# Walking the inner dimension of a fused attention and gated-MLP kernel in pairs of tiles

## The chip, the cores and the metric

One core of one Trainium2 chip runs the whole kernel in one launch. The metric is the device time in microseconds. A profile of one further execution gives the busy times, waits and transfers. Five engines run side by side: TensorE (PE, with its weight loads shown as PEld), VectorE (DVE), ScalarE (ACT), GpSimd (POOL) and SyncE (SP, which here only issues transfers).

## What is computed

Inputs are q, k and v for 8 batches, 8 heads, 576 positions and 64 features per head, and three weight matrices. Cut to what matters:

```python
# attention: a coarse part on means over 4 positions, and a local band of 7 positions
q_d, k_d, v_d = means of q, k, v over 4 neighbouring positions       # 144 positions
out_up    = repeat(softmax(q_d k_d^T / 8) v_d, 4)
out_local = softmax(mask(q k^T / 8, |i - j| < 4)) v
x = (out_up + out_local) as 4608 tokens of 512 features
# gated MLP
xn  = x / sqrt(mean(x^2) + 1e-6) * rms_g
g   = xn @ w_gate            # 512 x 1536
val = xn @ w_val             # 512 x 1536
out = (g * sigmoid(g) * val) @ w_out      # 1536 x 512
```

The weights arrive as 64-bit floats, which the kernel decodes on the chip.

## The kernel before

**Tokens.** The 4608 tokens are worked on in 18 chunks of 256 (C). For each chunk the class `Attention` computes the local band, adds the coarse result, normalises, and transposes the chunk on TensorE (`turn`, L907) into two tiles, `xh` (L911, ACT) and `xl` (L915, DVE): a rounded part and the remainder. Both come from the pool `xp`, with 2 buffers of each name. The class `Coarse` computes the coarse attention for two heads of one batch at a time; there are 32 such steps.

**The MLP.** The class `Forward` walks the inner dimension of 1536 in 12 tiles f of 128 (NF). For each f and each chunk:

- `first(f, 0)` and `first(f, 1)` (L976): 12 products of 128x256 each, which give gate and value in the two halves of one PSUM tile `ps_h` of 128x512 (3 buffers, one bank each);
- `tanh` (L983, ACT), `gate` (L986, DVE), `product` (L991, DVE), each on 128x256;
- `high` (L997, ACT) writes a rounded copy into the tile `hs`, `low` (L1000, DVE or POOL) the remainder;
- `second` (L1011): 6 products of 128x512 into two accumulators `ps_o`. It runs LAG = 2 tiles behind.

After f = 11 the two accumulators are copied (L1018) and stored (L1021). The buffers are `sil` 3 and `hs` LAG + 1 = 3.

**The weights.** Each of 36 pieces (512 KB of raw 64-bit numbers) goes through `fetch` (SP, L250), `scale` (ACT, L254, takes one of 4 `o_sb` buffers), `last_bits` (POOL, L264), `join` (DVE, L271), `high` (ACT, L281 or L283) and `split` (DVE, L293 or L295, or POOL, L291), which frees the `o_sb` buffer. A piece is of no use before all of these. 32 pieces are fetched into memory that later holds other weights; the pieces 28, 31, 34 and 35 are fetched into one extra tile `raw` of the pool `stage`, which holds one piece at a time. A staging place is free again after `join`. Pieces 24 to 31 hold the gate and value weights of the last four tiles f.

**What sets the order.** The opening is ordered by a planner written into the kernel (class `Plan`). Every step is a task with an engine, a cost, a due time and the buffers that it takes (`allocs`) or uses. At each turn the planner takes the task that can start earliest on its engine, and among those within 0.15 of it the one with the earliest due time. A task that takes a buffer can be picked only when all users of the buffer's earlier holder are planned (`room`). The instructions of each engine then stand in the planned order, in-order on the chip. The planner orders the opening attention, the weight pieces, and the chunks 0 to 2; from chunk 3 on a loop writes out one f after the other, with the steps of the next chunk's `Attention` and of `Coarse` placed between them at fixed fractions.

Three more places matter for what follows:

- `OpeningSums` adds up the sums for the coarse attention of the first two batches. For batch 1 it takes its results' places from the pools of the main loop: `xh` and `xl` for q and k (`load_qk`, `copy`, L420), two `hs` buffers for v (`add_v`, L429). The raw v lies where gate weights will be written, so the `high` step of gate and value pieces waits for the last `add_v`.
- `warm_up` (L1102) fills an `hs` buffer, on which 30 products without use (`idle_product`, L1105) keep TensorE busy. They are planned with the latest due times of all, so they run when TensorE has nothing else.
- `Attention.plan`: `turn(0)` takes `xh` and `xl`; the sums that chunk 1 makes on TensorE (`value_sum`, L827) wait for chunk 0's `turn`.

Of the kernel before, what the change touches and what calls it, by code (L numbers as in the profile page):

```python
# [8 lines left out]
FP32 = mybir.dt.float32  # L9
# [10 lines left out]
P = 128  # L20
# [13 lines left out]
US = 4  # L34
# [4 lines left out]
WPC = 512  # L39
LAG = 2  # L40
W_BUFS = 4
# [30 lines left out]
class Plan:  # L72
# [6 lines left out]
    def buf(self, res):  # L79
        return Buf(res)  # L80
# [90 lines left out]
def attn_moe_kernel(  # L171
# [73 lines left out]
    def load_weight(src, hi_lo, f, n, gain, k):  # L245
        st = {}

        def fetch(place):
            raw = st["raw"] = place if place is not None else stage.tile([P, WPC, 2], U32, name="raw")
            return nc.sync.dma_start(out=raw, in_=src.bitcast(U32).rearrange("p (n t) -> p n t", t=2)).ins  # L250
# [56 lines left out]
    def load_second(f):  # L307
# [56 lines left out]
    class OpeningSums:  # L364
# [57 lines left out]
        def add_v(self, j, engine):  # L422
            if j == 1:
                if self.b:
                    self.vs = ffn.tile([HALF, 4, 2, D], FP32, name="hs", bufs=LAG + 1)
# [3 lines left out]
            (nc.gpsimd if engine == "POOL" else nc.vector).tensor_tensor(  # L429
                out=vs, in0=self.raw_v[:, 0] if j == 1 else vs, in1=self.raw_v[:, j], op=ALU.add,  # L430
            )
# [153 lines left out]
    class Attention:  # L585
# [55 lines left out]
        def plan(self, newton="POOL", before=()):  # L641
# [98 lines left out]
        def load_score(self, j, par):  # L740
            k = load_kv(k_pad, 2 * self.c + j, par)
            if self.c == 0 and j == 1:
                q = ffn.tile([P, US, D], FP32, name="sil", bufs=3)
            else:
                q = loads.tile([P, US, D], FP32, name="q_t", bufs=2)
# [172 lines left out]
    class Forward:  # L918


        def __init__(self, att):
            self.att, self.c = att, att.c
            self.p, self.sil, self.hs, self.o_sb = {}, {}, {}, {}

        def emit(self, f):
            self.first(f, 0)
            self.first(f, 1)
            self.tanh(f)
            self.gate(f)
            self.product(f)  # L930
            self.high(f)
            self.low(f, "DVE")

        def emit_second(self, f):
            self.second(f)
            if f == NF - 1:
                for j in range(2):
                    self.copy(j)
                    self.store(j)

        def plan(self, weights, second_weights):
            att, c, T = self.att, self.c, due[self.c]
            o_bufs = [buf("ps_o") for _ in range(2)]
            last = None
            for f in range(NF):
                at = T + 4.2 * f
# [3 lines left out]
                first = task(  # L950
                    "PE", 1.375, lambda f=f: self.first(f, 0), at, [*att.turned, *weights(f)], allocs=[hp], uses=x,
                )
                tanh = task("ACT", 0.38, lambda f=f: self.tanh(f), soon, [first], allocs=[sil], uses=[hp])
                val = task("PE", 1.375, lambda f=f: self.first(f, 1), at, [first], uses=[hp, *x])
                gate = task("DVE", 0.415, lambda f=f: self.gate(f), soon, [tanh], uses=[hp, sil])
                prod = task("DVE", 0.415, lambda f=f: self.product(f), soon, [gate, val], uses=[hp, sil])
                high = task("ACT", 0.415, lambda f=f: self.high(f), soon, [prod], allocs=[hs], uses=[sil])
                low = task(
                    (("DVE", 0.42, soon), ("POOL", 0.95, soon)), 0, lambda e, f=f: self.low(f, e), soon, [high], uses=[sil, hs],
                )  # L960
                last = task(
                    "PE", 1.375, lambda f=f: self.second(f), at + 4.2 * LAG, [low, last, *second_weights(f)],
                    allocs=o_bufs if f == 0 else [], uses=[hs, *o_bufs],
                )
            for j in range(2):
# [3 lines left out]

        def first(self, f, t):  # L970
            if t == 0:
                self.p[f] = ps_h.tile([P, 2, C], FP32, name="ps_h")
            n, w = 0, (wg, wv)[t]
            for k in range(KT):
                for wi, xi in ((w[0], self.att.xh), (w[0], self.att.xl), (w[1], self.att.xh)):
                    nc.tensor.matmul(  # L976
                        out=self.p[f][:, t], lhsT=wi(f)[:, 0, k], rhs=xi[:, k], start=(n == 0), stop=(n == 3 * KT - 1),
                    )
                    n += 1

        def tanh(self, f):
            self.sil[f] = ffn.tile([P, C], FP32, name="sil", bufs=3)
            nc.scalar.activation(out=self.sil[f], in_=self.p[f][:, 0], func=AF.Tanh, scale=0.5)  # L983

        def gate(self, f):
            nc.vector.scalar_tensor_tensor(  # L986
                out=self.sil[f], in0=self.sil[f], scalar=1.0, in1=self.p[f][:, 0], op0=ALU.add, op1=ALU.mult,
            )

        def product(self, f):  # L990
            nc.vector.scalar_tensor_tensor(  # L991
                out=self.sil[f], in0=self.sil[f], scalar=0.5, in1=self.p[f][:, 1], op0=ALU.mult, op1=ALU.mult,
            )

        def high(self, f):
            self.hs[f] = ffn.tile([P, 2, C], FP32R, name="hs", bufs=LAG + 1)
            nc.scalar.activation(out=self.hs[f][:, 0], in_=self.sil[f], func=AF.Copy)  # L997

        def low(self, f, engine):
            (nc.gpsimd if engine == "POOL" else nc.vector).tensor_tensor(  # L1000
                out=self.hs[f][:, 1], in0=self.sil[f], in1=self.hs[f][:, 0], op=ALU.subtract,
            )

        def second(self, f):
            if f == 0:
                self.o = [ps_o.tile([P, DM], FP32, name="ps_o") for _ in range(2)]
            hh, hl = self.hs[f][:, 0], self.hs[f][:, 1]
            for j in range(2):
                cols = slice(j * P, (j + 1) * P)
                for i, (lhs, rhs) in enumerate(((hh, wo[0]), (hh, wo[1]), (hl, wo[0]))):  # L1010
                    nc.tensor.matmul(  # L1011
                        out=self.o[j], lhsT=lhs[:, cols], rhs=rhs(f)[:, 0],
                        start=(f == 0 and i == 0), stop=(f == NF - 1 and i == 2),
                    )
# [26 lines left out]
    spots = [f"first{n % 8}" for n in range(24)]  # L1041
    spots += ["second0", "second1", "second2", "second3", "stage", "second0", "second1", "stage"]
    spots += ["second2", "second3", "stage", "stage"]
    joined, whole = [], {}

    def decode(n):
# [4 lines left out]
        got = task(  # L1051
            "SP", 0.1, lambda: fetch(spot and spot[0].raw_place(*spot[1:])), at - 15, allocs=[raw],
            dma=0.524 * MB,
# [71 lines left out]
    for c in range(FIRST, NCH):  # L1125
# [10 lines left out]
        fwd = Forward(att)  # L1136
        for f in range(NF):
# [66 lines left out]
```

## Time and profile before

| What | Value |
|---|---|
| Time, median of 3 runs | 1144.62 us (1144.13 to 1148.87) |
| Span of the profiled execution | 1142.6 us |
| What lies around the span, against the median | 2.0 us |
| TensorE busy | 1080.1 us (95%) |
| VectorE busy | 963.1 us (84%) |
| ScalarE busy | 625.7 us (55%) |
| GpSimd busy | 173.0 us (15%) |
| First product of the MLP | at 107.84 us |
| Last copy out of the accumulators | at 1138.6 us |

No own time is listed for the profiled execution beside its span, so the median less the span stands for what lies around it.

How to read it: "L976" is line 976 of the kernel. A row of a group of instructions gives the line, the engine, the operation, output and inputs with their shapes, the count, then busy time and mean duration of one, then the engine's idle time before them and what ended it. A row of waits gives who waited for whom, the total, the number of times and the longest. A row of the timeline gives start and duration. A row of the table by stretches gives the length, then for each engine busy time and number of instructions, then the TensorE clock that was granted (1.00 is full), the share of the transfer engines and GB/s.

### The profile page before, as it was taken

The numbers are of one execution on the slowest core, as the hardware profiler recorded it, in microseconds if no ns is written. First come the engines' busy times: TensorE is split into PE (matmuls) and PEld (weight loads), VectorE is DVE, ScalarE is ACT, GpSimd is POOL, SyncE is SP. The second block draws the span as 40 slices with busy tenths as digits, with TensorE's granted clock in tenths as the row PEclk, the third lists the DMA queues.
The fourth block names the chain that finished last, engine by engine and source line by source line (L and its number), as shares of the span: only waits on it lengthen the run. The fifth ranks groups of instructions, "written<-read, shape, count | busy, mean of one in ns | idle before, by whom it ended". The sixth has DMA issues, their size and how long they took to land.

```text
span 1142.6 us, 21949 instructions
## 1 busy us (share of the span) xinstructions
PE 1080.1 (95%) x8002; PEld 987.1 (86%) x8002; DVE 963.1 (84%) x1869; ACT 625.7 (55%) x2284; POOL 173.0 (15%) x205
## 2 busy tenths in 40 slices
PE   6883799999999999999999999999999999999998
PEld 4772688878898899999999999998999999999997
DVE  6786998788999989797989797979898989997432
ACT  1564663847383847474747474747465573838221
POOL 1654662334200010101010101000000000000000
PEclk8875999999999899999999999999999999999999
DMA  9986482446544443535253535222231313220000
GB/s 267 300 274 173 107 222 84 96 95 148 124 100 105 110 104 88 115 88 115 83 120 88 114 88 114 78 63 76 65 89 54 99 52 99 67 60 20 1 19 20
DMA packets 76813, 119.57 MB, mean 105 GB/s; under 512 B 26784, under 2 KB 36256, under 8 KB 76704
## 3 DMA queue, kind: packets, MB, share of 16 engines
q1 hardware_dynamic: 47520, 97.34, 28.8%
q0 software_dynamic: 8640, 15.93, 9.1%
q10 hardware_dynamic: 20544, 4.89, 2.0%
q8 instruction: 63, 1.03, 0.4%
q14 instruction: 46, 0.38, 0.1%
HBM read 106.33 MB, written 11.80 MB: 103 GB/s over the span
## 4 chain that ended last, share of the span: by engine, by line
PE 78%; DVE 8%; DMA 7%; ACT 2%; issue 2%; POOL 1%; SPq 0%; ACTq 0%; DVEq 0%; POOLq 0%
PE ps_h L976 48%; PE ps_o L1011 24%; PE ps_a L541 2%; PE ps_a L499 2%; DMA wg<-in_v_sum_dram 1%; DMA wg<-in_w_gate_dram 1%; DVE o_sb L271 1%; PE ps_a L907 1%; DMA qk<-in_qk_sum_dram 1%; DMA kv<-in_k_pad_dram 1%; DVE prod L812 1%; PE ps_a L527 1%; DVE prod L758 1%; ACT up_t L856 1%; ACT prod L805 1%
## 5 line engine op out<-in xcount | busy, mean ns | idle before, releaser
L1011 PE MATMUL ps_o<-wo,hs 128*128 128x512 f32 x1296 | 355.7, 399 | 5.4 <-POOL hs L1000 5.3
L976 PE MATMUL ps_h<-xh,wg 128*128 128x256 f32 x1728 | 349.1, 282 | 4.0 <-DVE wg L295 1.7
L976 PE MATMUL ps_h<-xh,wv 128*128 128x256 f32 x1728 | 341.8, 280 | 5.0 <-DVE sil L986 4.9
L976 PEld LDWEIGHTS ps_h<-xh,wg 128*128 128x128 f32 x1728 | 284.0, 190 | 13.0 <-ACT xh L911 2.2
L976 PEld LDWEIGHTS ps_h<-xh,wv 128*128 128x128 f32 x1728 | 280.5, 188 | 11.0 <-DVE sil L986 6.9
L805 ACT ACTIVATE prod<-kv,sc 128x64 f32<-128x64 f32 x1072 | 279.2, 405 | 18.1 <-DVE x_t L831 9.8
L1011 PEld LDWEIGHTS ps_o<-wo,hs 128*128 128x128 f32 x1296 | 221.2, 188 | 43.1 <-POOL hs L1000 8.4
L976 PE MATMUL ps_h<-xl,wg 128*128 128x256 f32 x864 | 243.5, 282 | 0.1
L976 PE MATMUL ps_h<-xl,wv 128*128 128x256 f32 x864 | 241.8, 280 | 0.0
L983 ACT ACTIVATE sil<-ps_h 128x256 f32<-128x256 f32 x216 | 82.4, 382 | 227.8 <-PE ps_h L976 216.0
L986 DVE SCALAR_TENSOR_TENSOR sil<-sil,ps_h 128x256 f32<-128x256 f32 x216 | 91.1, 422 | 94.9 <-ACT sil L983 83.5
L976 PEld LDWEIGHTS ps_h<-xl,wg 128*128 128x128 f32 x864 | 164.0, 190 | 6.9 <-DVE sil L986 1.3
L976 PEld LDWEIGHTS ps_h<-xl,wv 128*128 128x128 f32 x864 | 163.0, 189 | 1.6
L997 ACT ACTIVATE hs<-sil 128x256 fp32r<-128x256 f32 x216 | 89.3, 415 | 133.9 <-DVE sil L991 112.3
L758 DVE TENSOR_TENSOR prod<-q_t,kv 128x896 f32<-128x896 f32 x140 | 153.1, 1094 | 5.7 <-DMA q_t<-in_q_band_dram 5.4
L762 DVE TENSOR_REDUCE sc<-prod 128x14 f32<-128x896 f32 x144 | 155.3, 1085 | 0.4
L831 DVE TENSOR_REDUCE x_t<-prod 128x128 f32<-128x896 f32 x128 | 135.7, 1080 | 11.5 <-PE ps_a L907 4.5
L812 DVE TENSOR_TENSOR prod<-sc,kv 128x384 f32<-128x384 f32 (+2 forms) x144 | 119.6, 868 | 0.2
L1000 DVE TENSOR_TENSOR hs<-sil,hs 128x256 fp32r<-128x256 f32 x196 | 87.3, 447 | 23.3 <-ACT hs L997 23.2
L991 DVE SCALAR_TENSOR_TENSOR sil<-sil,ps_h 128x256 f32<-128x256 f32 x216 | 91.2, 422 | 6.4 <-PE ps_h L976 4.8
L362 POOL DMA_DIRECT2D qk<-in_qk_sum_dram x36 | 32.2, 894 | 319.6 <-DMA qk<-in_qk_sum_dram 275.1
L856 ACT ACTIVATE up_t<-x_t 128x128 f32<-128x128 f32 x144 | 44.2, 307 | 21.3 <-DVE x_t L846 12.7
(118 smaller groups left out, 974.7 us busy)
## 6 DMA issues: line engine op xcount, KB each, us to landing
kv<-in_k_pad_dram SPq DMA_DIRECT2D x72, 320.0 KB
kv<-in_v_pad_dram SPq DMA_DIRECT2D x72, 320.0 KB
qk<-in_qk_sum_dram POOLq DMA_DIRECT2D x36, 288.0 KB, 5.0
out_dram<-o_sb SPq DMA_DIRECT2D x36, 256.0 KB
q_t<-in_q_band_dram SPq DMA_DIRECT2D x70, 128.0 KB
vs<-in_v_sum_dram POOLq DMA_DIRECT2D x36, 144.0 KB, 3.6
qk<-in_qk_sum_dram SPq DMA_DIRECT2D x12, 288.0 KB
wo<-in_qk_sum_dram SPq DMA_DIRECT2D x2, 1152.0 KB
```

Source lines behind the costliest of these rows:

```text
L758: nc.vector.tensor_tensor(out=pr, in0=bcast(q[:, s0:s0 + 2], 2, NO), in1=window(k, s0), op=ALU.mult)
L762: nc.vector.tensor_reduce(out=self.sc[:, j, par, s0:s0 + 2], in_=self.pr[i], axis=AX.X, op=ALU.add,)
L805: nc.scalar.activation(out=self.pr[i][:, o, s], in_=self.v[j, par][:, s0 + s + o], func=AF.Copy, scale=p[:, s, o:o + 1],)
L812: (nc.vector if engine == "DVE" else nc.gpsimd).tensor_tensor(out=self.pr[i][:, a:b], in0=bcast(p[:, :, a:b].rearrange("p s o -> p o s"), ...
L831: nc.vector.tensor_reduce(out=self.x[j][:, s0:s0 + 2, par], in_=pr.rearrange("p o s d -> p s d o"), axis=AX.X, op=ALU.add,)
L976: nc.tensor.matmul(out=self.p[f][:, t], lhsT=wi(f)[:, 0, k], rhs=xi[:, k], start=(n == 0), stop=(n == 3 * KT - 1),)
L983: nc.scalar.activation(out=self.sil[f], in_=self.p[f][:, 0], func=AF.Tanh, scale=0.5)
L986: nc.vector.scalar_tensor_tensor(out=self.sil[f], in0=self.sil[f], scalar=1.0, in1=self.p[f][:, 0], op0=ALU.add, op1=ALU.mult,)
L991: nc.vector.scalar_tensor_tensor(out=self.sil[f], in0=self.sil[f], scalar=0.5, in1=self.p[f][:, 1], op0=ALU.mult, op1=ALU.mult,)
L997: nc.scalar.activation(out=self.hs[f][:, 0], in_=self.sil[f], func=AF.Copy)
L1000: (nc.gpsimd if engine == "POOL" else nc.vector).tensor_tensor(out=self.hs[f][:, 1], in0=self.sil[f], in1=self.hs[f][:, 0], op=ALU.subtract,)
L1011: nc.tensor.matmul(out=self.o[j], lhsT=lhs[:, cols], rhs=rhs(f)[:, 0], start=(f == 0 and i == 0), stop=(f == NF - 1 and i == 2),)
```

## The change

The inner dimension is walked in 6 pairs n of tiles f = 2n and 2n + 1. The gates of both tiles share one `ps_h` bank and the values of both share another, so tanh, gate, product, `high` and `low` each work on 128x512 at once. The products themselves are the same in number and shape. LAG is 1 pair, `sil` and `hs` have 2 buffers of double width. In the loop from chunk 3 on, the 24 gate products of a pair come first, then other steps, then the 24 value products, then the `second` of the pair before. The extra tile `raw` and its pool go; the pieces 28 and 34 are fetched into a buffer of `xl`, 31 and 35 into one of `xh`. The second `turn` of a chunk now waits for the first.

```diff
-LAG = 2
+LAG = 1
...
-    stage = ctx.enter_context(tc.tile_pool(name="stage", bufs=1))
...
-            raw = st["raw"] = place if place is not None else stage.tile([P, WPC, 2], U32, name="raw")
+            raw = st["raw"] = place if not isinstance(place, str) else xp.tile([P, WPC, 2], U32, name=place)
...
-        "up_t": 2, "xh": 2, "xl": 2, "sil": 3, "hs": LAG + 1, "o_sb": W_BUFS, "ps_h": 3, "ps_o": 2, "ps_a": 3,
-        "rms": 1, **{f"first{i}": 1 for i in range(8)}, **{f"second{i}": 1 for i in range(4)}, "stage": 1,
+        "up_t": 2, "xh": 2, "xl": 2, "sil": 2, "hs": 2, "o_sb": W_BUFS, "ps_h": 3, "ps_o": 2, "ps_a": 3,
+        "rms": 1, **{f"first{i}": 1 for i in range(8)}, **{f"second{i}": 1 for i in range(4)},
...
-                    "PE", 0.6, lambda j=j: self.turn(j), T - 7 - TAIL, [norm],
+                    "PE", 0.6, lambda j=j: self.turn(j), T - 7 - TAIL, [norm, *self.turns],
...
+        def emit_gate(self, n):
+            for i in range(2):
+                self.first(n, i, 0)
+
+        def emit_value(self, n):
+            for i in range(2):
+                self.first(n, i, 1)
+            self.tanh(n)
+            self.gate(n)
+            self.product(n)
+            self.high(n)
+            self.low(n, "DVE")
...
-                hp, sil, hs = buf("ps_h"), buf("sil"), buf("hs")
+                gp, vp, sil, hs = buf("ps_h"), buf("ps_h"), buf("sil"), buf("hs")
...
-                    (("DVE", 0.42, soon), ("POOL", 0.95, soon)), 0, lambda e, f=f: self.low(f, e), soon, [high], uses=[sil, hs],
+                    (("DVE", 0.68, soon), ("POOL", 1.75, soon)), 0, lambda e, n=n: self.low(n, e), soon, [high], uses=[sil, hs],
...
-            self.sil[f] = ffn.tile([P, C], FP32, name="sil", bufs=3)
-            nc.scalar.activation(out=self.sil[f], in_=self.p[f][:, 0], func=AF.Tanh, scale=0.5)
+            self.sil[n] = ffn.tile([P, 2, C], FP32, name="sil")
+            nc.scalar.activation(out=self.sil[n], in_=self.g[n], func=AF.Tanh, scale=0.5)
...
-            self.hs[f] = ffn.tile([P, 2, C], FP32R, name="hs", bufs=LAG + 1)
+            self.hs[n] = ffn.tile([P, 2, 2, C], FP32R, name="hs")
...
-    spots += ["second0", "second1", "second2", "second3", "stage", "second0", "second1", "stage"]
-    spots += ["second2", "second3", "stage", "stage"]
+    spots += ["second0", "second1", "second2", "second3", "xl", "second0", "second1", "xh"]
+    spots += ["second2", "second3", "xl", "xh"]
...
-        t = ffn.tile([P, 2, C], FP32R, name="hs", bufs=LAG + 1)
+        t = ffn.tile([P, 2, C], FP32R, name="hs")
...
-        for f in range(NF):
-            fwd.emit(f)
-            late.append((fwd, f))
-            if len(late) > LAG:
-                fw, g = late.pop(0)
-                fw.emit_second(g)
-            while todo and todo[0][0] < f + 1:
-                todo.pop(0)[1]()
+        for n in range(NF // 2):
+            for half in range(2):
+                (fwd.emit_value if half else fwd.emit_gate)(n)
+                if half:
+                    late.append((fwd, n))
+                    if len(late) > LAG:
+                        fw, g = late.pop(0)
+                        fw.emit_second(g)
+                while todo and todo[0][0] < 2 * n + half + 1:
+                    todo.pop(0)[1]()
```

More of the change, by code (lines that the diff above doesn't have):

```diff
@@ L424, in add_v @@
                 if self.b:
-                    self.vs = ffn.tile([HALF, 4, 2, D], FP32, name="hs", bufs=LAG + 1)
+                    self.vs = ffn.tile([HALF, 4, 2, D], FP32, name="hs")
                 else:
@@ L742, in load_score @@
             if self.c == 0 and j == 1:
-                q = ffn.tile([P, US, D], FP32, name="sil", bufs=3)
+                q = ffn.tile([P, US, D], FP32, name="sil")
             else:
@@ L922, in __init__, with emit_second @@
             self.att, self.c = att, att.c
[L923 to L936, printed above, removed]
+            self.g, self.v, self.sil, self.hs, self.o_sb = {}, {}, {}, {}, {}
+        def emit_gate(self, n):
[9 more added lines that the diff above has]
+            self.low(n, "DVE")
+        def emit_second(self, n):
+            for i in range(2):
+                self.second(n, i)
+            if n == NF // 2 - 1:
                 for j in range(2):
@@ L944, in plan @@
             last = None
-            for f in range(NF):
-                at = T + 4.2 * f
+            for n in range(NF // 2):
+                at = T + 8.4 * n
                 soon = at - SOON
-                hp, sil, hs = buf("ps_h"), buf("sil"), buf("hs")
+                gp, vp, sil, hs = buf("ps_h"), buf("ps_h"), buf("sil"), buf("hs")
                 x = [att.xh_buf, att.xl_buf]
-                first = task(
-                    "PE", 1.375, lambda f=f: self.first(f, 0), at, [*att.turned, *weights(f)], allocs=[hp], uses=x,
-                )
[L953 to L958, printed above, removed]
-                    (("DVE", 0.42, soon), ("POOL", 0.95, soon)), 0, lambda e, f=f: self.low(f, e), soon, [high], uses=[sil, hs],
[L960 to L964, printed above, removed]
@@ new lines, in plan @@
+                gates, vals = [], []
+                for i in range(2):
+                    gates.append(task(
+                        "PE", 1.375, lambda n=n, i=i: self.first(n, i, 0), at, [*att.turned, *weights(2 * n + i), *gates],
+                        allocs=[gp] if i == 0 else [], uses=[gp, *x],
+                    ))
+                for i in range(2):
+                    vals.append(task(
+                        "PE", 1.375, lambda n=n, i=i: self.first(n, i, 1), at, [*gates, *vals],
+                        allocs=[vp] if i == 0 else [], uses=[vp, *x],
+                    ))
@@ new lines, in plan @@
+                tanh = task("ACT", 0.6, lambda n=n: self.tanh(n), soon, gates, allocs=[sil], uses=[gp])
+                gate = task("DVE", 0.68, lambda n=n: self.gate(n), soon, [tanh], uses=[gp, sil])
+                prod = task("DVE", 0.68, lambda n=n: self.product(n), soon, [gate, *vals], uses=[vp, sil])
+                high = task("ACT", 0.6, lambda n=n: self.high(n), soon, [prod], allocs=[hs], uses=[sil])
+                low = task(
+                    (("DVE", 0.68, soon), ("POOL", 1.75, soon)), 0, lambda e, n=n: self.low(n, e), soon, [high], uses=[sil, hs],
+                )
@@ L965, in plan @@
+                for i in range(2):
+                    last = task(
+                        "PE", 1.375, lambda n=n, i=i: self.second(n, i), at + 8.4 * LAG, [low, last, *second_weights(2 * n + i)],
+                        allocs=o_bufs if n == i == 0 else [], uses=[hs, *o_bufs],
+                    )
             for j in range(2):
@@ L968, in plan, with first @@
                 task("SP", 0.1, lambda j=j: self.store(j), T, [copy], uses=[o_sb], dma=0.256 * MB)
[L970 to L973, printed above, removed]
+        def first(self, n, i, t):
+            p = (self.g, self.v)[t]
+            if i == 0:
+                p[n] = ps_h.tile([P, 2, C], FP32, name="ps_h")
+            f, m, w = 2 * n + i, 0, (wg, wv)[t]
             for k in range(KT):
@@ L985, in gate, with tanh @@
-        def gate(self, f):
+                    m += 1
+        def tanh(self, n):
+            self.sil[n] = ffn.tile([P, 2, C], FP32, name="sil")
+            nc.scalar.activation(out=self.sil[n], in_=self.g[n], func=AF.Tanh, scale=0.5)
+        def gate(self, n):
             nc.vector.scalar_tensor_tensor(
-                out=self.sil[f], in0=self.sil[f], scalar=1.0, in1=self.p[f][:, 0], op0=ALU.add, op1=ALU.mult,
+                out=self.sil[n], in0=self.sil[n], scalar=1.0, in1=self.g[n], op0=ALU.add, op1=ALU.mult,
@@ L988, in gate, with product @@
             )
-        def product(self, f):
+        def product(self, n):
             nc.vector.scalar_tensor_tensor(
-                out=self.sil[f], in0=self.sil[f], scalar=0.5, in1=self.p[f][:, 1], op0=ALU.mult, op1=ALU.mult,
+                out=self.sil[n], in0=self.sil[n], scalar=0.5, in1=self.v[n], op0=ALU.mult, op1=ALU.mult,
             )
-        def high(self, f):
-            self.hs[f] = ffn.tile([P, 2, C], FP32R, name="hs", bufs=LAG + 1)
-            nc.scalar.activation(out=self.hs[f][:, 0], in_=self.sil[f], func=AF.Copy)
@@ L999, in low, with high @@
-        def low(self, f, engine):
+        def high(self, n):
+            self.hs[n] = ffn.tile([P, 2, 2, C], FP32R, name="hs")
+            nc.scalar.activation(out=self.hs[n][:, 0], in_=self.sil[n], func=AF.Copy)
+        def low(self, n, engine):
             (nc.gpsimd if engine == "POOL" else nc.vector).tensor_tensor(
-                out=self.hs[f][:, 1], in0=self.sil[f], in1=self.hs[f][:, 0], op=ALU.subtract,
+                out=self.hs[n][:, 1], in0=self.sil[n], in1=self.hs[n][:, 0], op=ALU.subtract,
@@ L1011, in second @@
                     nc.tensor.matmul(
                         out=self.o[j], lhsT=lhs[:, cols], rhs=rhs(f)[:, 0],
-                        start=(f == 0 and i == 0), stop=(f == NF - 1 and i == 2),
+                        start=(f == 0 and m == 0), stop=(f == NF - 1 and m == 2),
                     )
@@ L1051, in decode @@
         got = task(
-            "SP", 0.1, lambda: fetch(spot and spot[0].raw_place(*spot[1:])), at - 15, allocs=[raw],
+            "SP", 0.1, lambda: fetch(spot[0].raw_place(*spot[1:]) if spot else spots[n]), at - 15, allocs=[raw],
             dma=0.524 * MB,
```

13 lines of the change are left out of this document (6 added, 7 removed).

## The prediction

> **What bounds the kernel now.** I read the busy slices of the page first, then the busy time by stretch, then TensorE's own waits.
>
> ```profile
> span 1142.6 us, 21949 instructions
> PE   6883799999999999999999999999999999999998
> DVE  6786998788999989797989797979898989997432
> PEclk8875999999999899999999999999999999999999
> ...
> 0.00:44.00 44.00, 29.77 (x154) 23.78 (x155) 31.04 (x42) 10.01 (x34) 11.74 (x13) 0.88 0.96 266
> 44.00:60.00 16.00, 15.32 (x130) 12.90 (x130) 12.95 (x23) 12.21 (x39) 13.31 (x14) 0.91 1.02 338
> 60.00:92.00 32.00, 21.99 (x182) 18.98 (x180) 28.48 (x49) 19.26 (x59) 19.80 (x18) 0.72 0.87 270
> 92.00:108.00 16.00, 2.92 (x11) 2.09 (x11) 9.71 (x23) 7.98 (x25) 7.21 (x9) 0.50 0.53 170
> 108.00:147.00 39.00, 32.28 (x218) 28.84 (x219) 34.37 (x54) 25.05 (x55) 21.40 (x21) 0.95 0.52 122
> 147.00:186.00 39.00, 35.87 (x266) 32.85 (x265) 35.49 (x62) 21.84 (x64) 18.41 (x20) 1.00 0.57 153
> 186.00:392.00 206.00, 195.66 (x1498) 176.72 (x1496) 180.53 (x339) 125.68 (x497) 50.07 (x78) 0.98 0.47 109
> 392.00:1094.00 702.00, 702.00 (x5243) 649.92 (x5242) 617.04 (x1251) 393.36 (x1491) 31.09 (x36) 1.00 0.32 81
> 1094.00:1142.60 48.60, 44.33 (x314) 40.99 (x312) 13.49 (x32) 10.31 (x25) 0.00 (x0) 1.00 0.06 23
> ```
>
> From 392 to 1094 TensorE is busy for all of 702 us at full clock. Nothing that only eases VectorE or ScalarE can shorten that stretch, as the change leaves every product as it is. What can move lies ahead of it. From 108 on, TensorE has 32.28 + 35.87 + 195.66 + 702 + 44.33 = 1010.1 us of work; its idle time there is 6.7 (to 147), 3.1 (to 186), 10.3 (to 392) and 4.3 at the end. So the end is the moment when the MLP starts, plus 1010, plus 20.2 of gaps, plus 4.3. The gaps can be won; the start can be lost.
>
> ```profile
> 105.00 2.17 PE L907 MATMUL ps_a<-ident_sb,x_t 128*128 128x128 f32 x8 [3.74 <-DVE x_t L895]
> 107.84 0.58 PE L976 MATMUL ps_h<-xh,wg 128*128 128x256 f32 x1 [0.68 <-ACT xh L911]
> ...
> PE ps_h L976 <- DVE sil L986: 4.9, 5, 2.4
> ```
>
> The first product (L976) starts 2.84 us after chunk 0's `turn` (L907).
>
> **Part 1: the wide steps.** The steps with the costs to compare:
>
> ```profile
> L983 ACT ACTIVATE sil<-ps_h 128x256 f32<-128x256 f32 x216 | 82.4, 382 | 227.8 <-PE ps_h L976 216.0
> L986 DVE SCALAR_TENSOR_TENSOR sil<-sil,ps_h 128x256 f32<-128x256 f32 x216 | 91.1, 422 | 94.9 <-ACT sil L983 83.5
> L997 ACT ACTIVATE hs<-sil 128x256 fp32r<-128x256 f32 x216 | 89.3, 415 | 133.9 <-DVE sil L991 112.3
> L1000 DVE TENSOR_TENSOR hs<-sil,hs 128x256 fp32r<-128x256 f32 x196 | 87.3, 447 | 23.3 <-ACT hs L997 23.2
> L991 DVE SCALAR_TENSOR_TENSOR sil<-sil,ps_h 128x256 f32<-128x256 f32 x216 | 91.2, 422 | 6.4 <-PE ps_h L976 4.8
> ...
> L915 DVE TENSOR_TENSOR xl<-ps_a,xh 128x512 fp32r<-128x512 f32 x36 | 23.6, 684 | 0.2 <-ACT xh L911 0.2
> L911 ACT CAST xh<-ps_a 128x512 fp32r<-128x512 f32 x36 | 19.6, 586 | 11.1 <-PE ps_a L907 7.1 <-DMA up_t<-up 3.8
> ```
>
> For a 128x512 step I take 0.684 on VectorE (L915, also one PSUM input) and 0.586 on ScalarE. A pair of tiles cost VectorE 2 x (0.422 + 0.422 + 0.447) = 2.58 and will cost 3 x 0.684 = 2.05: 0.53 less, 57 us over 108 pairs, 9.6 over the 18 pairs of the opening's three chunks. ScalarE saves 2 x (0.382 + 0.415) - 2 x 0.586 = 0.42 a pair. Past 392 the products cover all of it, so it is worth nothing there; without that cover, it would be worth at most the 57.
>
> The Trainium skill (Perfetto Trace Analysis, Optimizing Scalar/DVE Operations) puts the saving per dropped VectorE instruction at about 60 ns on SBUF and 125 on PSUM: by it the pair saves an estimated 0.31, and the opening 5.6 instead of 9.6, and the time would come out some 3 us above mine. The rows above show more than the page, 0.53.
>
> Gate and value no longer share a bank. Five times, 4.9 us in all (L976 after L986), TensorE waited with the value products until VectorE had read the gate; that kind of wait goes. It is part of the 20.2.
>
> **Part 2: the staging places, where I expect the loss.** This trace has the pieces 28 and 31 as the first two users of `raw`:
>
> ```profile
> 74.26 0.59 SPq L250 DMA_DIRECT2D raw<-in_w_gate_dram  x1
> 84.90 0.33 SPq L250 DMA_DIRECT2D wg<-in_w_val_dram  x1
> ...
> 143.90 0.67 ACT L254 ACTIVATE o_sb<-raw 128x512 f32<-128x512 f32 x1
> ...
> 147.35 0.68 DVE L271 SCALAR_TENSOR_TENSOR o_sb<-o_sb,raw 128x512 uint32<-128x512 uint32 x1
> ...
> 67.59 0.71 PE L499 MATMUL ps_a<-xh 64*72 64x144 f32 x8
> 78.72 1.36 PE L499 MATMUL ps_h<-xl 64*72 64x144 f32 x8
> ```
>
> Piece 28 is fetched at 74.26, long before its turn (joined at 147.35), because SP has nothing more urgent: its next fetch is at 84.90. With places in `xl` and `xh`, 28 takes the free second `xl` at that moment and 31 the free second `xh` right behind it. The first `xh` is free once its last coarse scores are done (67.59 + 0.71), the first `xl` at 80.1; SP's gap up to 84.90 is where 35 and 34 go. All four places are then held by raw weights, before chunk 0's `turn` asks for one of each at 105. The planner gives a buffer only when its holder is through, so `turn` waits until 28 and 31 are joined. Behind it on TensorE stand the whole MLP of chunk 0 and chunk 1's sums (L827), which wait for chunk 0's `turn`; so nothing useful fills the wait.
>
> When are 28 and 31 joined? Pieces are decoded in order, since each needs one of four `o_sb` buffers and the earlier ones are due first. VectorE is the busy engine of that stretch, so I take its work:
>
> ```profile
> L1000 DVE TENSOR_TENSOR hs<-sil,hs 128x256 fp32r<-128x256 f32 x3 | 2.7, 910 | 0.0
> L991 DVE SCALAR_TENSOR_TENSOR sil<-sil,ps_h 128x256 f32<-128x256 f32 x6 | 2.5, 416 | 0.6 <-PE ps_h L976 0.6
> L986 DVE SCALAR_TENSOR_TENSOR sil<-sil,ps_h 128x256 f32<-128x256 f32 x6 | 2.4, 408 | 3.9 <-PE ps_h L976 2.4 <-ACT sil L983 1.5
> L915 DVE TENSOR_TENSOR xl<-ps_a,xh 128x512 fp32r<-128x512 f32 x2 | 1.3, 674 | 0.0
> ```
>
> Up to 147 it did 31.04 + 12.95 + 28.48 + 9.71 + 34.37 = 116.6. The MLP steps, which now can't run yet, were 2.7 + 2.5 + 2.4 + 1.3 = 8.9 of it (the four rows above, up to 147.4). Two joins of 0.68 come on top: 109.1. It was idle for 147 - 116.6 = 30.4, of which 3.9 + 0.6 was waiting for the MLP's products: 25.9 remain. 109.1 + 25.9 = 135.
>
> Part of the same is the `hs` buffer. With two instead of three, the second coarse v sum of batch 1 can't start before the idle products on the warm-up tile are through:
>
> ```profile
> 59.91 0.73 PE L1105 MATMUL ps_o<-hs 128*128 128x256 f32 x4
> ...
> 38.28 0.69 DVE L429 TENSOR_TENSOR hs<-wg 72x512 f32<-72x512 f32 x1 [1.99 <-DMA wg<-in_v_sum_dram]
> ...
> L283 ACT ACTIVATE wg<-o_sb,g_sb x12: 704/722/729, 48.5 to 152.5; 128x512 fp32r<-128x512 f32 x12
> ```
>
> The sum moves from 38.28 to 60.6, and three adds of 0.69 end at 62.7; the first gate piece's `high` (L283, at 48.5) waits for it: 14 later. Four pieces can be scaled and joined meanwhile and attention work fills VectorE (it was busy for 12.95 of those 16 us), so I take 3, between 0 and 14.
>
> So 31 is joined at 138 and the first product comes at 138 + 2.84 = 141, 33 later than now. Bounds: if all of VectorE's idle time after 44 (17.4 of the 30.4) is filled, 109.1 + 13.0 + 2.84 = 125, or 17 later; with the whole 14, 135 + 14 + 2.84 = 152, or 44 later.
>
> **What comes back.** Chunk 0 then finds its weights decoded or nearly so. The 6.7 + 3.1 of gaps before 186 go. Of the 10.3 behind it I take 7, since VectorE has 9.6 less to do and a longer lead. One of these gaps also cost clock:
>
> ```profile
> 374.00:386.00 12.00, 9.93 (x66) 9.29 (x67) 11.66 (x20) 11.85 (x52) 0.00 (x0) 0.72 0.34 104
> ```
>
> At 0.72 for 12 us that is up to 3.4; I take 2. Together 19 (bounds: 10, with only the gaps before 186; 24, with everything).
>
> **The end of the kernel** costs nothing: after the last value products come product, `high` and `low`, 0.684 + 0.586 + 0.684 = 1.95, against 12 products (L1011) of the pair before.
>
> ```profile
> 1134.05 4.29 PE L1011 MATMUL ps_o<-wo,hs 128*128 128x512 f32 x18
> ```
>
> 18 of them take 4.29, so 12 cover 2.9; a longer handover than 0.9 would show at the end alone.
>
> **Sum.** + 33 - 19 = + 14 on the profiled execution's 1142.6: 1156.6 of span. The median shown, 1144.62, lies 2.0 above that span, so the time is 1158.6, say 1159.
>
> **Rivals.**
>
> *Faster: the decoder runs ahead.* If pieces 28 and 31 are joined early enough, nothing is lost and the gaps are won. This decides at a first product at 121: the 19 that come back, less 5.7 (0.5%, about what a measurement of this kernel can tell from no change), is 13 after 107.84. For it: VectorE's 16 us at 92 to 108 were only 9.71 busy, and the MLP no longer competes. Against: even with all its idle time after 44 filled I get 125. At no delay at all, the full 19 give 1125.6; at a delay of 8, 1134.
>
> *The two cancel.* A first product at 121 to 133 ends within 5.7 of now: 1139 to 1150. The lower bound of 125 lies in it.
>
> *Nothing of it matters.* If the fetches of 31 and 34 came after `turn`, the opening would stay as it is and 1144.6 with it; the idle SP from 74.9 to 84.9 speaks against that.
>
> *The wide steps starve TensorE.* The skill page named above also says that where Vector and Scalar are not saturated but cause bubbles elsewhere, breaking instructions up lets work finish sooner, which speaks against this change. As a mechanism here: product to `low` takes 1.95 instead of 0.422 + 0.415 + 0.447 = 1.28 before `second` may start, 0.67 more; exposed in all 108 pairs this is 72, or 1217. But between the value products of a pair and its `second` lie 48 products of the next pair, and 702 us without a gap show that such cover held for single tiles. I give it 0.03.
>
> **How the numbers follow.** A first product after 133 and so slower by more than 0.5%: 0.60, with the starving case 0.63 (forecast 1159). Cancelled or without effect: 0.20. Decoder ahead: 0.17. The range reaches from a delay of 17 with 24 won, 1137.6, to 44 with only 10 won, 1178.6; I cut the upper end to 1174, as both extremes at once are unlikely, and set the lower one to 1137. The forecast's own range is 1150 to 1174.
>
> **What would show it.** In the changed profile: the fetches of 28, 31, 34 and 35 into `xl` and `xh` before 90; the first product (L976 before) at 125 to 152 and within 5 us behind the join of 31; TensorE idle for more than 30 us before it at half clock; VectorE's 128x512 steps near 0.68; fewer than 12 us of gaps between the first product and the steady stretch; the first gate `high` near 63. I am wrong if the first product stays near 108, if the gaps do not shrink, or if TensorE shows gaps in the steady loop.

## The result and the profile after

The changed kernel takes 1166.47 us (median of 4 runs, 1163.85 to 1167.34), the kernel before 1145.66 in the runs beside it (4 runs, 1144.13 to 1148.87). The ratio is 1.0163, 95% interval 1.0131 to 1.0195: slower by 1.6%. The profiled execution took 1167.34 us, 1.84 more than its span.

The page of the changed kernel, busy shares in 40 slices and TensorE's clock:

```profile
span 1165.5 us, 21372 instructions
PE   6880179999999999999999999999999999999998
DVE  6688978889785697979788979898988989897322
PEclk8885589999999999999999999999999999999999
```

The hole in TensorE's row sits in the fourth and fifth slice (87 to 146 us): it is deeper and longer than before, and the clock row shows half speed there. The steady part is as full as before. By stretch (busy time and count of PE, PEld, DVE, ACT, POOL; then clock, transfer share, GB/s):

```profile
92.00:108.00 16.00, 2.76 (x10) 1.93 (x10) 12.43 (x24) 8.07 (x24) 6.20 (x7) 0.50 0.43 114
108.00:147.00 39.00, 5.71 (x28) 5.52 (x28) 37.48 (x49) 26.33 (x47) 21.69 (x22) 0.54 0.69 189
147.00:186.00 39.00, 34.00 (x265) 32.67 (x266) 32.22 (x47) 18.78 (x58) 13.25 (x15) 0.92 0.46 101
186.00:392.00 206.00, 199.75 (x1510) 183.53 (x1508) 164.33 (x270) 106.30 (x393) 51.91 (x73) 0.98 0.43 100
392.00:1090.00 698.00, 698.00 (x5225) 650.02 (x5223) 613.46 (x1031) 390.01 (x1401) 31.09 (x36) 1.00 0.33 83
1090.00:1165.50 75.50, 71.69 (x510) 66.54 (x508) 20.07 (x32) 13.79 (x23) 0.00 (x0) 0.99 0.04 15
```

From 108 to 147 TensorE does 5.71 us of work where it did 32.28, and VectorE is busy for 37.48 of 39. What TensorE waits for, from its timeline in the changed kernel (start, duration, idle time before and what ended it):

```profile
102.73 2.17 PE L906 MATMUL ps_a<-ident_sb,x_t 128*128 128x128 f32 x8 [3.70 <-DVE x_t L894]
135.03 5.71 PE L826 MATMUL ps_a<-prod,ident_sb 128*128 128x128 f32 x28 [30.12 <-ACT prod L804]
150.21 0.58 PE L989 MATMUL ps_h<-xh,wg 128*128 128x256 f32 x1 [9.46 <-ACT xh L910]
```

Both `turn`s of chunk 0 (L906) run at 102.73, even a little earlier than before (105.00), since they need only a PSUM bank. What is late is the copy of their result into `xh` (L910). Ahead of it TensorE has 28 products of chunk 1's sums (L826), which wait 30.12; then it waits 9.46 more for `xh`. The first product comes at 150.21, 42.4 later than at 107.84. Who holds `xh` and `xl` is seen in the timelines of SP's queue and of VectorE in the changed kernel:

```profile
65.03 0.33 SPq L249 DMA_DIRECT2D xl<-in_w_gate_dram  x1
65.40 0.43 SPq L249 DMA_DIRECT2D xh<-in_w_val_dram  x1
70.92 0.33 SPq L249 DMA_DIRECT2D xh<-in_w_out_dram  x1
80.18 0.53 SPq L249 DMA_DIRECT2D xl<-in_w_out_dram  x1
```

```profile
140.07 0.68 DVE L270 SCALAR_TENSOR_TENSOR o_sb<-o_sb,xl 128x512 uint32<-128x512 uint32 x1
...
144.25 0.68 DVE L270 SCALAR_TENSOR_TENSOR o_sb<-o_sb,xh 128x512 uint32<-128x512 uint32 x1
```

All four places are taken by raw weights before 81. Piece 28 is joined at 140.07, 31 at 144.25, and only then may `xh` be written. ScalarE's timeline shows the last step of the wait:

```profile
146.75 0.66 ACT L253 ACTIVATE o_sb<-wo 128x512 f32<-128x512 f32 x1 [2.33 <-DMA wo<-in_w_out_dram]
147.31 0.71 ACT L282 ACTIVATE wv<-o_sb,g_sb 128x512 fp32r<-128x512 f32 x1
147.93 0.57 ACT L910 CAST xh<-ps_a 128x512 fp32r<-128x512 f32 x1
```

The copy stands in ScalarE's order behind the `scale` of a later piece, and that waits 2.33 for its transfer. From the start of the join to the first product it is 5.96 us, against the 2.84 from `turn` to first product before.

The books close on the spans. The first product is 42.4 later. Behind it TensorE idles for 1.8 to 186 (39 less 34.00, less the 3.2 before the first product), 6.25 to 392 and 3.8 at the end, 11.9 in all, where it idled for 24.5 before. And its work behind that point is 1003.4 (from 147) instead of 1010.1 (from 108). So 42.4 - 12.6 - 6.7 = 23.1, against 22.9 between the spans.

### The profile page after: what moved, and what is told of

Same layout as the page of the kernel before. It is cut to its first block, busy times and chain, and to the rows that moved or that the text cites. A ratio compares the mean times of both kernels' runs of the same rounds, so it can differ in the third digit from the quotient of the medians.

```text
span 1165.5 us, 21372 instructions
## 1 busy us (share of the span) xinstructions
PE 1078.3 (93%) x8002; PEld 995.1 (85%) x8002; DVE 946.5 (81%) x1557; ACT 601.6 (52%) x2068; POOL 161.9 (14%) x193
## 4 chain that ended last, share of the span: by engine, by line
PE 83%; DMA 5%; DVE 5%; ACT 3%; issue 2%; SPq 1%; POOL 1%; ACTq 0%; DVEq 0%; POOLq 0%
PE ps_h L989 50%; PE ps_o L1025 25%; PE ps_a L540 2%; DMA vs<-in_v_sum_dram 2%; PE ps_a L498 2%; DMA kv<-in_v_pad_dram 2%; PE ps_a L906 1%; PE ps_a L526 1%; DVE o_sb L270 1%; ACT prod L804 1%; PE ps_o L826 1%; DMA wo<-in_w_out_dram 1%; SPq L401 1%; DVE prod L757 1%; DMA kv<-in_k_pad_dram 1%
## 5 line engine op out<-in xcount | busy, mean ns | idle before, releaser
L1025 PE MATMUL ps_o<-wo,hs 128*128 128x512 f32 x1296 | 334.4, 399 | 5.9 <-POOL hs L1013 5.9
L989 PE MATMUL ps_h<-xh,wg 128*128 128x256 f32 x1728 | 326.9, 281 | 9.5 <-ACT xh L910 9.5
L989 PE MATMUL ps_h<-xh,wv 128*128 128x256 f32 x1728 | 326.2, 282 | 0.0
L989 PEld LDWEIGHTS ps_h<-xh,wg 128*128 128x128 f32 x1728 | 274.5, 189 | 16.0 <-ACT xh L910 9.7
L989 PEld LDWEIGHTS ps_h<-xh,wv 128*128 128x128 f32 x1728 | 273.2, 189 | 3.9 <-issue 2.3
L1025 PEld LDWEIGHTS ps_o<-wo,hs 128*128 128x128 f32 x1296 | 232.9, 190 | 50.0 <-POOL hs L1013 7.4
L1010 ACT ACTIVATE hs<-sil 128x512 fp32r<-128x512 f32 x108 | 68.0, 630 | 177.3 <-DVE sil L1004 165.9
L996 ACT ACTIVATE sil<-ps_h 128x512 f32<-128x512 f32 x108 | 64.4, 596 | 162.0 <-PE ps_h L989 151.5
L999 DVE SCALAR_TENSOR_TENSOR sil<-sil,ps_h 128x512 f32<-128x512 f32 x108 | 73.8, 683 | 59.6 <-ACT sil L996 59.2
L1004 DVE SCALAR_TENSOR_TENSOR sil<-sil,ps_h 128x512 f32<-128x512 f32 x108 | 74.4, 689 | 34.3 <-PE ps_h L989 34.2
L1013 DVE TENSOR_TENSOR hs<-sil,hs 128x512 fp32r<-128x512 f32 x98 | 67.2, 686 | 18.3 <-ACT hs L1010 18.3
```

The source lines that it names most:

```text
L989: nc.tensor.matmul(out=p[n][:, i], lhsT=wi(f)[:, 0, k], rhs=xi[:, k], start=(m == 0), stop=(m == 3 * KT - 1),)
L996: nc.scalar.activation(out=self.sil[n], in_=self.g[n], func=AF.Tanh, scale=0.5)
L999: nc.vector.scalar_tensor_tensor(out=self.sil[n], in0=self.sil[n], scalar=1.0, in1=self.g[n], op0=ALU.add, op1=ALU.mult,)
L1004: nc.vector.scalar_tensor_tensor(out=self.sil[n], in0=self.sil[n], scalar=0.5, in1=self.v[n], op0=ALU.mult, op1=ALU.mult,)
L1010: nc.scalar.activation(out=self.hs[n][:, 0], in_=self.sil[n], func=AF.Copy)
L1025: nc.tensor.matmul(out=self.o[j], lhsT=lhs[:, cols], rhs=rhs(f)[:, 0], start=(f == 0 and m == 0), stop=(f == NF - 1 and m == 2),)
```

## The experiments

Eleven kernels, in the order in which they ran. "Behind it" is the span of the profiled execution less the start of the first MLP product. The ratio is to the runs of the kernel before that were made beside each kernel (medians 1145.66 to 1147.37 us). The last two columns come from one profiled execution each, and that can lie some us off the median: 1152.77 us in e2, 1135.62 in e4, 1155.72 in e7.

| Kernel | Time, us | Ratio to before, 95% | First product | Behind it |
|---|---|---|---|---|
| before | 1145.66 | 1 | 107.84 | 1034.8 |
| after | 1166.47 | 1.0163 [1.0131, 1.0195] | 150.21 | 1015.3 |
| e1 before + places | 1165.11 | 1.0155 [1.0120, 1.0189] | 145.82 | 1018.1 |
| e2 after, one place | 1148.13 | 1.0003 [0.9985, 1.0021] | 112.90 | 1038.1 |
| e3 after, 26 idle products | 1164.51 | 1.0150 [1.0114, 1.0187] | 145.29 | 1015.2 |
| e4 = e2 and e3 | 1141.03 | 0.9950 [0.9931, 0.9969] | 106.02 | 1027.8 |
| e5 = e3, fetched late | 1144.83 | 0.9973 [0.9951, 0.9995] | 107.57 | 1036.0 |
| e6 before, 26 idle products | 1149.34 | 1.0020 [0.9999, 1.0041] | 108.22 | 1036.8 |
| e7 before, `turn`s in order | 1150.24 | 1.0021 [0.9997, 1.0044] | 112.67 | 1041.2 |
| e8 after, `low` on VectorE | 1155.38 | 1.0068 [1.0044, 1.0092] | 146.74 | 1004.6 |
| e9 e4, `low` on VectorE | 1148.59 | 0.9999 [0.9977, 1.0021] | 109.46 | 1040.3 |
| e10 e5, `low` on VectorE | 1147.84 | 1.0008 [0.9991, 1.0025] | 105.86 | 1039.7 |
| e11 before, `low` on VectorE | 1156.57 | 1.0083 [1.0052, 1.0113] | 109.50 | 1045.3 |

My theory was that the held places cost the time. The rivals were the wide steps, the two `hs` buffers, the sharing of the tiles as such, and POOL's wide `low`.

**e1: the places alone.** The kernel before, with the four staged pieces in `xl` and `xh` and the dependency between the `turn`s; all steps stay 128x256, `hs` stays at 3.

```diff
-    spots += ["second0", "second1", "second2", "second3", "stage", "second0", "second1", "stage"]
-    spots += ["second2", "second3", "stage", "stage"]
+    spots += ["second0", "second1", "second2", "second3", "xl", "second0", "second1", "xh"]
+    spots += ["second2", "second3", "xl", "xh"]
```

> The kernel before (single tiles, three hs buffers) with only the staging places moved from the extra tile to xl and xh. Held places: the turn of chunk 0 waits for the joins of pieces 28 and 31, so the first product comes at 140 to 152 instead of 108, and the time is 1160 to 1172. Rival, the pairs themselves (wide steps, LAG of one pair) cost the time: first product near 108, 1145.

TensorE's timeline in e1:

```profile
132.07 5.37 PE L826 MATMUL ps_a<-prod,ident_sb 128*128 128x128 f32 x28 [22.74 <-ACT prod L804]
145.82 0.58 PE L975 MATMUL ps_h<-xh,wg 128*128 128x256 f32 x1 [8.39 <-ACT xh L910]
```

The same two waits, in the same order, without a single wide step. The time is that of the change: 1.0155 against 1.0163. One more thing is in e1's table by stretch:

```profile
147.00:186.00 39.00, 37.12 (x265) 35.11 (x266) 27.41 (x49) 15.90 (x55) 12.97 (x16) 0.92 0.39 81
186.00:392.00 206.00, 200.07 (x1523) 182.92 (x1523) 168.60 (x330) 113.15 (x436) 48.44 (x75) 0.99 0.44 101
```

The gaps behind a late first product are small here too (1.9 and 5.9). So most of what comes back needs no wide steps. Weights that are decoded by then are only a part of it: in before, TensorE waited 2.4 us for weights behind the first product.

```profile
PE ps_h L976 <- DVE wg L295: 1.7, 1, 1.7
PE ps_h L976 <- ACT wg L283: 0.7, 1, 0.7
```

No such wait is left in e1. The wait for POOL's `low` shrank more, from 5.3 to 1.4 (lines of e1):

```profile
PE ps_h L975 <- DVE sil L985: 3.9, 6, 1.1
PE ps_o L1010 <- POOL hs L999: 1.4, 1, 1.4
```

**e2: one place.** The kernel after, with the four pieces one after the other through one buffer of `xl`, so that chunk 0's `turn` finds the other `xl` and both `xh` free.

```diff
+    held = []
+
+    def staged():
+        if not held:
+            held.append(xp.tile([P, WPC, 2], U32, name="xl"))
+        return held[0]
...
-            raw = st["raw"] = place if not isinstance(place, str) else xp.tile([P, WPC, 2], U32, name=place)
+            raw = st["raw"] = place if not isinstance(place, str) else staged()
```

> The changed kernel, but all four pieces go one after the other through a single buffer of xl, as they did through the extra tile; the other xl and both xh stay free for chunk 0. Held places: the first product is back at 106 to 114, and with the gaps that the pairs win the span is 1130 to 1139. Rival, the pairs themselves cost the time: it stays above 1155. Rival, the decoder on VectorE is the cause whatever holds the places: the first product stays at 135 or later.

The first product is back at 112.90 and the loss is gone. The span of 1151.0 missed the 1130 to 1139 that I expected: I had counted on keeping the 19 that "come back". Most of that was lost again in gaps, which are 26.5 us in all behind the first product, where after has 11.9 and before 24.5. The weights are not ready earlier than before; the second to fourth staged pieces are joined at 166 to 179, in before at 156 to 172.

**e3: fewer idle products.** The kernel after with 26 idle products on the `hs` buffer instead of 30 (`range(30)` becomes `range(26)`), so that the buffer is free for the coarse sum sooner.

> The changed kernel with 26 idle products instead of 30, so that the warm-up buffer of hs is free at about 21 and not at 61. My sum gave the hs wait 3 us of the first product's delay: first gate high near 48 instead of 63, first product at 147, time 1163. Rival, the hs wait is most of the delay: first product at 138 or earlier. Rival, it is nothing: 150 as now.

What was to be freed, in the timeline of the changed kernel:

```profile
61.30 1.10 PE L1119 MATMUL ps_o<-hs 128*128 128x256 f32 x4
62.44 0.69 DVE L428 TENSOR_TENSOR hs<-wg 72x512 f32<-72x512 f32 x1 [0.49 <-PE ps_o L1119]
...
64.17 0.72 ACT L282 ACTIVATE wg<-o_sb,g_sb 128x512 fp32r<-128x512 f32 x1
```

The last idle products hold `hs` up to 62.4, and the first gate `high` comes at 64.17. With 26 products it comes at 49.0, and the first product at 145.29, 4.9 earlier. In time, 1164.51 and 1166.47 can't be told apart. Held against e1, e3 shows what the pairs are worth with the places held and the `hs` hold gone: 1.0150 against 1.0155, no difference that can be told.

**e4: both.** One place and 26 idle products.

> Both of the last two edits. Held places with the hs term of 3 us: first product 0 to 4 us ahead of that with one place alone, span 1128 to 1138. If the hs wait matters only through the staging places, it is the same as with one place alone.

```profile
106.02 0.58 PE L996 MATMUL ps_h<-xh,wg 128*128 128x256 f32 x1 [0.87 <-ACT xh L917]
```

This is the fastest kernel of the study, 0.5% under before, with the first product (the line above, TensorE's timeline) at 106.02. That is 6.9 ahead of e2, more than the 0 to 4 that I expected. The span of 1133.8 lies in the expected range, but it belongs to the fastest of ten executions. In e2 the hold put the first gate `high` at 72.1; here it is at 48.6.

**e5: fetched late.** The kernel of e3, places in `xl` and `xh` as in the change, but the fetch of a staged piece may be planned only behind chunk 0's `turn`s.

```diff
-            "SP", 0.1, lambda: fetch(spot[0].raw_place(*spot[1:]) if spot else spots[n]), at - 15, allocs=[raw],
-            dma=0.524 * MB,
+            "SP", 0.1, lambda: fetch(spot[0].raw_place(*spot[1:]) if spot else spots[n]), at - 15,
+            [] if spot else atts[0].turns, allocs=[raw], dma=0.524 * MB,
```

> The kernel of e3 (after, with 26 idle products), but the four staged pieces may only be fetched once chunk 0's two `turn`s are done. The places stay in `xl` and `xh`, the steps stay wide. My theory (the loss is that the staged pieces hold the buffers before `turn` needs them): the fetches of 28 and 31 move from 65 us to behind 100, the first product moves from 145.3 to 104 to 112, and the long wait before it is gone; pieces 28 to 35 then come later, so that forward 0 waits for weights or chunk 1 for its `xl`: 5 to 15 us more of gaps than e3 after the first product. Time 1133 to 1150. Rival (the shared tiles or the wide steps cost the time, whenever the pieces are fetched): 1155 or more.

SP's queue and TensorE in e5:

```profile
101.46 0.55 SPq L249 DMA_DIRECT2D xl<-in_w_gate_dram  x1
106.10 0.33 SPq L249 DMA_DIRECT2D xh<-in_w_val_dram  x1
```

```profile
107.57 0.58 PE L989 MATMUL ps_h<-xh,wg 128*128 128x256 f32 x1 [0.86 <-ACT xh L910]
```

The dependency holds in the planner's order, which sets who gets which buffer; on the chip the fetch of 28 starts at 101.46, a little ahead of the `turn`s. The same tiles, shared in the same way, cost nothing once chunk 0 has its buffers before the raw weights get theirs: 1144.83 against e3's 1164.51, for one dependency. The first product moved by 37.7, the time by 19.7. In the spans, 20.8 of the 37.7 were lost again behind the first product: 6.3 in gaps, as expected, and 14.5 in TensorE's work, at a granted clock of 0.96 up to 392, where e3 has 0.98.

**e6 and e7: two small edits of the kernel before.** e6 has 26 idle products. e7 has only the dependency of the second `turn` on the first (`[norm, *self.turns]`).

> The kernel before, with 26 idle products instead of 30 and nothing else. My theory (the idle products cost only where two `hs` buffers must serve them, the coarse sum and the opening; before has three): first gate `high` stays at 48 to 50, the time within 0.3% of before, 1142 to 1149. Rival (fewer idle products are worth the 0.5% by themselves, so that e4's gain over before is not the wide steps'): 1136 to 1141.

> The kernel before, with the change's one dependency alone: the second `turn` of a chunk is planned after the first. My theory: it reorders some of the opening but holds nothing, first product between 104 and 113, time within 0.4%: 1141 to 1150; so e1's loss is the places' alone. Rival (this dependency has a share of e1's 19 us): first product at 118 or later, 1153 or more.

Neither is faster, and both end 0.2 to 0.3 us above the range that I gave. e6 rules out that fewer idle products gain by themselves in the kernel before. In e7 the planner writes out another order of the opening, and the first product comes at 112.67. With a ratio of 1.0021, at most 1.0044, it isn't what costs e1 its 19 us.

**e8 to e11: POOL's `low`.** In the kernel after, output products wait for a 128x512 `low` on POOL, three times, 5.9 us in all:

```profile
PE ps_o L1025 <- POOL hs L1013: 5.9, 3, 3.4
```

Two of the three, 5.3 us, lie between 186 and 392, where all gaps together are 6.25. Each of the four kernels keeps `low` on VectorE in the opening:

```diff
-                    (("DVE", 0.68, soon), ("POOL", 1.75, soon)), 0, lambda e, n=n: self.low(n, e), soon, [high], uses=[sil, hs],
+                    "DVE", 0.68, lambda n=n: self.low(n, "DVE"), soon, [high], uses=[sil, hs],
```

> The kernel after, with the `low` of the opening's three chunks on VectorE alone, so that no product waits for a 128x512 `low` of 1.6 us on POOL. If the new waits of 5.9 us (output products for POOL's `low`) lie on the path: they go, and the time falls by 3 to 6 from 1166.5, to 1160 to 1164, first product still at 146 to 153. Rival (TensorE's wait moves to another step, as the planner's order and VectorE's load shift): 1165 to 1169 with as much of gaps between 147 and 392 as after, 8 us.

> The kernel of e4 (wide steps, the four staged pieces one after the other through one `xl`, 26 idle products), with the `low` of the opening's three chunks on VectorE alone as in e8. If e8's 11 us came from TensorE's waits for POOL's wide `low`: e4's trace shows none of those waits, so nothing is left to win, 1138 to 1144. If they came from the planner's order, or from POOL's shorter list as such: some 5 to 11 us less than e4's 1141, 1130 to 1136.

> The kernel of e5 (wide steps, the staged pieces fetched behind chunk 0's `turn`s, 26 idle products), with the `low` of the opening's three chunks on VectorE alone. e5's trace names no wait for POOL's `low` among its larger waits, so by my theory the time stays at e5's 1144.8 within 4 us: 1141 to 1149; if low on VectorE is a gain whatever the rest, 1134 to 1140. First product at 104 to 110 in both.

> The kernel before, with the `low` of the opening's three chunks on VectorE alone. It has 5 waits of 5.3 us for POOL's narrow `low`. If those waits are exposed, they go: 1140 to 1144; then e9 and e10 have to be held against this kernel and not against before. Rival (the wide `low` of 1.6 us is what costs, the narrow one of 0.9 doesn't): 1145 to 1149, no difference. First product at 104 to 112 in both.

Only e10 came out as expected (1147.84, first product 105.86). e8, e9 and e11 lie outside both of the ranges that I gave them. Seen alone, e8 looks like a find: 11.1 us faster than after, more than the waits were long. But the same edit makes e4 slower by 7.6, e5 by 3.0 and before by 10. TensorE's waits in e11 and in before show a part of it:

```profile
PE ps_o L1011 <- DVE hs L1000: 3.3, 4, 2.1
```

```profile
PE ps_o L1011 <- POOL hs L1000: 5.3, 5, 1.4
```

Before had waits for POOL's `low` too. Without them the output products wait for VectorE's `low`, and the planner orders the opening anew (piece 28 is joined at 150.78, in before at 147.35). So e8 doesn't show that the wide `low` on POOL costs 11 us. What the four show together is a scatter: the same edit moves the time by -11 to +10 us. I put that down to the planner's order; no run separates the order from the rest. A difference of that size between two of these kernels proves no mechanism, and that holds for e4's gain over before as well: 5.4 us were measured, but e9, which has all of e4's edits and one more, is 0.9999.

## Why the prediction was right, step by step

**The bound and the place of the loss: right.** TensorE is busy for 698 of 698 us past 392 with wide steps too, so the starving case is out there. The end still follows the first product. Pieces 28, 31, 34 and 35 took the places at 65 to 81, of which I had read 74 to 85 from SP's idle time. One detail was wrong: I had `turn` itself waiting for the joins, but it ran at 102.73, and the copy into `xh` waited. e1 shows that the places alone cost 19 us, e5 that they cost nothing when fetched late. That is the rival "nothing of it matters" brought about on purpose; its condition, a fetch behind `turn`, was the right one, and so was its time, that of before: e5 takes 0.9973 of it. In the four kernels with held places (after, e1, e3, e8) no first product came before 145, so neither "decoder runs ahead" nor "the two cancel" (121 to 133) was near.

**The delay: 42.4, not 33.** This is the term of the sum that was too small. I had 109.1 of VectorE work, 25.9 idle, 3 for the `hs` hold and 2.84 of handover. VectorE's busy time up to the start of the join of 31 at 144.25, in the changed kernel (the last line of a table of five stretches; only the sum matters):

```profile
sum 144.25, DVE 115.07; mean DVE 23.01
```

The work was 6.0 more than I took. I had put two joins on top of what was done before, those of 28 and 31, and left out that 29 and 30 are decoded in between, although I had said that the order is kept. VectorE's groups up to this moment show it: three more joins than before up to 147, which with some longer ones took 4.3 us instead of 1.4, three more `split`s (2.1), and 1.0 more for the sums of v (L428); the steps of chunk 1's attention took no more than before. The idle time was 29.2, against 25.9 + 3; the handover was 5.96, as ScalarE's order put a waiting `scale` ahead of the copy. 6.0 + 0.3 + 3.1 = 9.4, which is the miss. Of the signs that I had listed, the one on the handover failed: the first product came 5.96 us behind the start of the join, and I had written within 5. The `hs` hold was seen rightly (first gate `high` at 64.17, 63 forecast); e3 puts its part in the first product at 4.9 where I took 3, and e8, with the hold, lies only 1.5 above e3, so that it is known no better than 1.5 to 5.

**"Nothing useful fills the wait": wrong by a little.** 28 products of chunk 1's sums ran in it. Behind the first product, where before has them, 28 such products take 3.4 us (L827, up to 147). That is half of the 6.7 us of TensorE work that were gone from there. For the other 3.3 I have no cause: the granted clock behind the first product is 0.98 up to 392 in both kernels, so the 2 that I took for the clock are not seen.

**What comes back: the size right by luck, the cause wrong.** I took 19; 12.6 of gaps and 6.7 of work are 19.3. The terms don't match: I had 9.8 of gaps before 186, 7 behind and 2 for the clock, and the runs gave 8.0, 4.1, 0.5 at the end and 6.7 of work. And I put it down in part to VectorE's 9.6 us less of work in the opening. e1 gets back 16.7 (1034.8 less 1018.1) with narrow steps. Over all kernels, a first product at 145 to 150 leaves 1005 to 1018 behind it, one at 106 to 113 leaves 1028 to 1045. So it goes with the delay. My reading is that whatever else has to be ready goes on being made while TensorE waits; no run tests that by itself. What stayed of the gaps was a term that I hadn't taken up: POOL's wide `low`, at 1.62 us a step where the narrow one took 0.89.

**The wide steps: 0.16 a pair, not 0.53.** The durations were as forecast. The groups of the changed kernel:

```profile
L1004 DVE SCALAR_TENSOR_TENSOR sil<-sil,ps_h 128x512 f32<-128x512 f32 x108 | 74.4, 689 | 34.3 <-PE ps_h L989 34.2
L999 DVE SCALAR_TENSOR_TENSOR sil<-sil,ps_h 128x512 f32<-128x512 f32 x108 | 73.8, 683 | 59.6 <-ACT sil L996 59.2
L1013 DVE TENSOR_TENSOR hs<-sil,hs 128x512 fp32r<-128x512 f32 x98 | 67.2, 686 | 18.3 <-ACT hs L1010 18.3
```

The three rows sum to 215.4, where those of before summed to 269.6: 54.2 less, as forecast. Yet VectorE's busy time fell by only 17.4 from e1 to after (963.9 to 946.5), which share the places and differ in the width; 17.4 over 108 pairs is 0.16. Over all kernels, the five with narrow steps average 962.0 and the eight with wide ones 942.2, which makes 0.18. The sum of durations counts twice what neighbours overlap. Two steps back to back, in VectorE's timeline of before and of after:

```profile
703.28 0.42 DVE L986 SCALAR_TENSOR_TENSOR sil<-sil,ps_h 128x256 f32<-128x256 f32 x1 [0.76 <-ACT sil L983]
703.62 1.66 DVE L812 TENSOR_TENSOR prod<-sc,kv 128x384 f32<-128x384 f32 x2
```

```profile
703.42 0.68 DVE L1004 SCALAR_TENSOR_TENSOR sil<-sil,ps_h 128x512 f32<-128x512 f32 x1
704.02 0.41 DVE L553 TENSOR_TENSOR o_g<-ps_a,z_g 72x256 f32<-72x256 f32 x1
```

A 128x256 step lasts 0.42, but the next one starts 0.34 later; a 128x512 step lasts 0.68 and the next starts 0.60 later. From 392 to 1090 the same distances hold for some 380 narrow steps (medians of 0.33 to 0.34) and 195 wide ones (0.60) that another step followed without a wait; where the next step reads the result, `product` behind `gate` in before, it is 0.46. From start to start a pair costs 6 x 0.34 = 2.04 and then 3 x 0.60 = 1.80: 0.24 instead of 0.53. The Trainium skill (Perfetto Trace Analysis, Optimizing Scalar/DVE Operations), by which I had estimated 0.31, is nearer than my rows were, though above what was measured: 317 VectorE instructions fewer (1874 to 1557) gave 55 ns each. The Trainium skill adds in the same section that part of a profiled duration, the write acknowledgement, overlaps with the next instruction; the 0.08 us here agree with that, and I had not applied it to my rows. In the opening's 18 pairs that is 3 to 4 us, not 9.6. Whether it reaches the time can't be seen: without held places the wide kernels (e2, e4, e5, e9, e10) leave 1028 to 1040 behind the first product, the narrow ones (before, e6, e7, e11) 1035 to 1045, and single kernels scatter by as much.

**The gate and value banks: right.** The wait of value products for `gate` is no longer among TensorE's waits in the changed kernel; it was 4.9 us in all before. e1, which starts as late but has narrow steps, still has 3.9 of it (its line is shown above), so it went with the pairs.

## What to carry to other kernels

Staging raw data in the main loop's spare buffers costs nothing in memory, but each such buffer is held from its fetch to its last reader, and a queue with nothing more urgent fetches early: ask who needs the buffer next, and tie the fetch to that user (one dependency was worth 20 us here) rather than to free space. Cost a VectorE step by the distance from its start to the next one's in a full stretch (here 0.34 and 0.60), not by its duration (0.42 and 0.68). Where a planner writes out the order, as here, run a few edits without meaning to learn its scatter first, and believe only what is larger.

## What was not expected of the hardware

Neighbouring VectorE steps overlap in the records by about 0.08 us at both widths, so grouping steps saved less than their durations say. The wait that was predicted at `turn` showed up behind it: TensorE's transposes had run 47 us before the first product, into PSUM, and it was ScalarE's copy out of PSUM that stood still. A wait has to be looked for at the instruction that writes the held buffer. The granted clock stayed at 0.54 through the 39 us in which TensorE did 5.71 of work, and had risen to 0.92 in the mean of the next 39.
